# Top-chunk attention and an MLP block on one core: fp16 split selection, constant rows kept in rings, LayerNorm folded into W1, and an order of work written by hand

## The chip, the cores and the metric

The kernel runs on one core of a Trainium2 chip. The metric is the device time of one execution in microseconds (us). TensorE is PE in the profile (its weight loads PEld), VectorE is DVE, ScalarE is ACT, GpSimd is POOL, SyncE is SP. A clock of 1.00 is the full granted clock of TensorE.

## The reference, cut to what matters

There are 4 batches, 8 heads, 768 positions and a head size of 64. Keys are grouped in 24 chunks of 32 positions.

```python
k_min, k_max = min/max of k over each chunk                # per head: 24 x 64
ub = sum_d max(q * k_min, q * k_max)                       # 768 x 24 upper bounds
ub = where(chunk of q >= chunk, ub, -1e9)                  # causal
top = the 6 chunks with the largest ub, for each q
scores = q @ k.T / 8, kept where the key's chunk is in top and key <= query
x = softmax(scores) @ v                                    # heads side by side: 768 x 512
xn = (x - mean(x)) / sqrt(var(x) + 1e-6) * g_ln
out = x + max(xn @ w_ch1, 0) @ w_ch2                       # 512 -> 2048 -> 512
```

Inputs and the output are float32.

## The kernel before

Heads are worked on in pairs; pair g has two heads of one batch, and there are 16 pairs, four to a batch. A pair passes three stages, and then the batch passes a fourth:

- `prep_pair` loads q, k and v, transposes q and k on PE in f32 (L193), and copies q as f32 and as fp16 (L207, L219, L220). It splits q in its positive and its negative part, `Q1` and `Q2` (L223, L224), takes the chunk maxima and minima of k (L213, L214), and puts them in block-diagonal `K1` and `K2`. The fp16 operands `qst` and `kst` of a head have 128 rows: 64 of data, 24 of a chunk mask, and zeros. DVE copies the constant rows anew for each pair (L238 to L245).
- `select_pair` forms the bounds with two f32 matmuls for each of five row tiles (L259, L260; the first 128 rows need no selection). DVE adds the causal bias (L262), finds the largest eight of 24 for each row and head (L269), compares with the seventh (L271), and makes a mask of 0 and -240 (L276). PE transposes the mask (L282, L285) and DVE copies it into the mask rows of `qst` (L288, L289). The score matmul then adds it without another instruction.
- `attend_head` computes the scores transposed, in eight pieces of up to 512 columns (L301), with Exp on ACT (L305). DVE zeroes the upper triangle of the six diagonal blocks (L308), 21 matmuls with v and a column of ones give values and denominators (L313), and DVE normalises (L318, L319).
- `mlp_batch` does LayerNorm row tile by row tile (L331 to L344: statistics, Sqrt on ACT, subtract and scale, transpose), the first product with Relu (L354, L358), the second (L363), the residual add (L368), and the store on POOL's queue (L371).

The weights are loaded and converted by two DMAs on POOL's queue when pair 0 has been prepared, and DVE scales the first by `g_ln` (L153). The outer loop prepares pair g+2, selects pair g+1, attends pair g; when a batch is complete, its MLP follows the attention of the next batch's first pair. Within that, a scheduler orders each engine's instructions. In the shipped order the four scalings of L153 stand in DVE's queue ahead of the rest of the selection of pair 0.

Of the kernel before, what the change touches and what calls it, by code (L numbers as in the profile page):

```python
# [18 lines left out]
def kernel(  # L20
# [9 lines left out]
):  # L30
    nc = tc.nc
# [3 lines left out]
    assert D == 64 and S % P == 0 and H % 2 == 0  # L35
    CH = 32
    NCH = S // CH
    NT = S // P
    HP = H // 2
    SCALE = 1.0 / math.sqrt(D)  # L40
    DM = H * D
    HID = moe_w_ch1.shape[1]
    assert moe_w_ch1.shape[0] == DM and tuple(moe_w_ch2.shape) == (HID, DM)
    KT1 = DM // P
    KT2 = HID // P
    MT1 = HID // P
    LN_EPS = 1e-6
    NEGBIG = -2.0e9
    NEGM = 240.0
    MR = 32  # L50
    assert NCH <= 24 and NT >= 2

    KA = 64 + MR

    const = ctx.enter_context(tc.tile_pool(name="const", bufs=1))
    wpool = ctx.enter_context(tc.tile_pool(name="wpool", bufs=1))
    qkn = ctx.enter_context(tc.tile_pool(name="qkn", bufs=3))
    vp = ctx.enter_context(tc.tile_pool(name="vp", bufs=1))
    pw = ctx.enter_context(tc.tile_pool(name="pw", bufs=3))
    stk = ctx.enter_context(tc.tile_pool(name="stk", bufs=H))  # L60
    vap = ctx.enter_context(tc.tile_pool(name="vap", bufs=3))
    selp = ctx.enter_context(tc.tile_pool(name="selp", bufs=3))
    ptp = ctx.enter_context(tc.tile_pool(name="ptp", bufs=2))
    xp = ctx.enter_context(tc.tile_pool(name="xp", bufs=2))
    lnp = ctx.enter_context(tc.tile_pool(name="lnp", bufs=2))
    xntp = ctx.enter_context(tc.tile_pool(name="xntp", bufs=2))
# [3 lines left out]
    ps_tr = ctx.enter_context(tc.tile_pool(name="ps_tr", bufs=2, space=bass.MemoryType.PSUM))  # L70
    ps_sm = ctx.enter_context(tc.tile_pool(name="ps_sm", bufs=2, space=bass.MemoryType.PSUM))
    ps_sc = ctx.enter_context(tc.tile_pool(name="ps_sc", bufs=3, space=bass.MemoryType.PSUM))
    ps_h = ctx.enter_context(tc.tile_pool(name="ps_h", bufs=1, space=bass.MemoryType.PSUM))

    ident_f = const.tile([P, P], F32, name="ident_f", tag="ident_f")
    make_identity(nc, ident_f)
    ident_h = const.tile([P, P], F16, name="ident_h", tag="ident_h")
    make_identity(nc, ident_h)

    Lmask = const.tile([P, P], F16, name="Lmask", tag="Lmask")  # L80
    nc.gpsimd.memset(Lmask, 1.0)
    nc.gpsimd.affine_select(
        out=Lmask, in_=Lmask, compare_op=ALU.is_ge, fill=0.0,
        base=0, pattern=[[1, P]], channel_multiplier=-1,
    )

    def build_R(tile_rows_base):
        rc = const.tile([tile_rows_base + MR, S], F16, name=f"Rc{tile_rows_base}", tag=f"Rc{tile_rows_base}")
        r = rc[tile_rows_base:tile_rows_base + MR, :]
        nc.gpsimd.memset(r, 0.0)  # L90
        rr = rc[tile_rows_base:tile_rows_base + NCH, :]
        nc.gpsimd.memset(rr, 1.0)
        nc.gpsimd.affine_select(  # L93
            out=rr, in_=rr, compare_op=ALU.is_ge, fill=0.0,
            base=0, pattern=[[1, S]], channel_multiplier=-CH,
        )
        nc.gpsimd.affine_select(
            out=rr, in_=rr, compare_op=ALU.is_ge, fill=0.0,
            base=CH - 1, pattern=[[-1, S]], channel_multiplier=CH,
        )  # L100
        return rc

    Rc64 = build_R(64)
    Rc0 = build_R(0)

    causb = const.tile([P, NT - 1, NCH], F32, name="causb", tag="causb")
    nc.gpsimd.memset(causb, 0.0)
    GPC = P // CH
    for s in range(1, NT):
        for g in range(GPC):  # L110
            nc.gpsimd.affine_select(
                out=causb[g * CH:(g + 1) * CH, s - 1, :],
                in_=causb[g * CH:(g + 1) * CH, s - 1, :],
                compare_op=ALU.is_ge, fill=NEGBIG,
                base=s * GPC + g, pattern=[[-1, NCH]], channel_multiplier=0,
            )

    mneg0 = const.tile([P, MR], F16, name="mneg0", tag="mneg0")
    nc.gpsimd.memset(mneg0, 0.0)
    for g in range(GPC):  # L120
        nc.gpsimd.affine_select(
            out=mneg0[g * CH:(g + 1) * CH, 0:NCH],
            in_=mneg0[g * CH:(g + 1) * CH, 0:NCH],
            compare_op=ALU.is_ge, fill=-NEGM,
            base=g, pattern=[[-1, NCH]], channel_multiplier=0,
        )
    mT0A = const.tile([P, P], F16, name="mT0A", tag="mT0A")
    mT0B = const.tile([P, P], F16, name="mT0B", tag="mT0B")
    ps0 = ps_h.tile([P, 5 * P], F16, name="sel_ps", tag="sel_ps")
    nc.tensor.transpose(ps0[64:64 + MR, 0:P], mneg0, ident_h, tile_position=(0, 64))  # L130
    nc.tensor.transpose(ps0[0:MR, P:2 * P], mneg0, ident_h, tile_position=(0, 0))
    nc.vector.tensor_copy(mT0A[64:64 + MR, :], ps0[64:64 + MR, 0:P])
    nc.vector.tensor_copy(mT0B[0:MR, :], ps0[0:MR, P:2 * P])

    z32 = const.tile([P, S], F16, name="z32", tag="z32")
    nc.gpsimd.memset(z32[0:MR, :], 0.0)

    eps_t = const.tile([P, 1], F32, name="eps_t", tag="eps_t")
    nc.vector.memset(eps_t, LN_EPS)

    wstate = {}

    def load_weights():
        if wstate:
            return
        w1b = wpool.tile([P, KT1, HID], F16, name="w1b", tag="w1b")
        nc.gpsimd.dma_start(w1b, moe_w_ch1.rearrange("(kt p) n -> p kt n", p=P))
        w2b = wpool.tile([P, KT2, DM], F16, name="w2b", tag="w2b")
        nc.gpsimd.dma_start(w2b, moe_w_ch2.rearrange("(kt p) n -> p kt n", p=P))
        gstr = wpool.tile([P, KT1], F32, name="gstr", tag="gstr")  # L150
        nc.sync.dma_start(gstr, moe_g_ln.rearrange("(kt p) -> p kt", p=P))
        for kt in range(KT1):
            nc.vector.tensor_scalar(  # L153
                w1b[:, kt, :], w1b[:, kt, :], gstr[:, kt:kt + 1], None, op0=ALU.mult,
            )
        wstate["w1b"] = w1b
        wstate["w2b"] = w2b
# [6 lines left out]
    def col_chunks(t):  # L164
        res = []
        c0 = P * t
        while c0 < S:
            cw = min(512, S - c0)
            res.append((c0, cw))
            c0 += cw  # L170
        return res

    def prep_pair(b, hp):
        hA = 2 * hp
        qn_t = qkn.tile([P, NT, 2, D], F32, name="qn_t", tag="qn_t")
        kn_t = qkn.tile([P, NT, 2, D], F32, name="kn_t", tag="kn_t")
        for hh in range(2):
            nc.sync.dma_start(qn_t[:, :, hh, :], q_r[b, :, :, hA + hh])
            nc.sync.dma_start(kn_t[:, :, hh, :], k_r[b, :, :, hA + hh])

        qstA = stk.tile([P, S], F16, name="qst", tag="qst")
        qstB = stk.tile([P, S], F16, name="qst", tag="qst")
        kstA = stk.tile([P, S], F16, name="kst", tag="kst")
        kstB = stk.tile([P, S], F16, name="kst", tag="kst")

        def transposes_and_evacs(src_t, stA, stB, fcopy_tile=None, red=None, cast_eng=None):
            cast_eng = cast_eng or nc.vector
            t0 = 0
            while t0 < NT:
                nb = min(4, NT - t0)  # L190
                pst = ps_tr.tile([P, 4 * P], F32, name="tr_ps", tag="tr_ps")
                for tt in range(nb):
                    nc.tensor.transpose(  # L193
                        pst[:, tt * P:(tt + 1) * P], src_t[:, t0 + tt, :, :], ident_f,
                    )
                c0 = t0 * P
                cw = nb * P
                if stA is None:
                    pass
                elif cast_eng is nc.scalar:  # L200
                    nc.scalar.copy(stA[0:64, c0:c0 + cw], pst[0:64, 0:cw])
                    nc.scalar.copy(stB[64:P, c0:c0 + cw], pst[64:P, 0:cw])
                else:
                    cast_eng.tensor_copy(stA[0:64, c0:c0 + cw], pst[0:64, 0:cw])
                    cast_eng.tensor_copy(stB[64:P, c0:c0 + cw], pst[64:P, 0:cw])
                if fcopy_tile is not None:
                    nc.scalar.copy(fcopy_tile[:, c0:c0 + cw], pst[:, 0:cw])  # L207
                if red is not None:
                    kmp, kmn = red
                    cc0 = c0 // CH  # L210
                    ccn = cw // CH
# [36 lines left out]
        for hh in range(2):  # L248
            nc.gpsimd.dma_start(va[:, hh, :, 0:D], v_r[b, :, :, hA + hh])  # L249
# [125 lines left out]
    def get_x_all(bb):  # L375
        if bb not in x_tiles:
            x_tiles[bb] = xp.tile([P, NT, H, D], F16, name="x_all", tag="x_all")
# [76 lines left out]
```

The softmax here doesn't subtract the row's maximum and nothing guards it: scores larger than these inputs give would overflow.

## Time and profile before

| | |
|---|---|
| median of 3 runs | 455.45 us (453.67 to 456.37) |
| profiled execution | the page gives its span, 453.3 us; no other time of it is given |
| mean granted clock of PE | 0.902 |
| busy PE / DVE / ACT / POOL | 368.0 / 261.2 / 208.3 / 69.1 us |
| first score matmul | 45.72 us |
| a pair, without MLP | 13.7 to 13.8 us |
| LayerNorm of batch 0 | 114.5 to 124.3 us |
| MLP products of batch 0 | 124.3 to 144.9 and 144.9 to 166.0 us |

The span runs from the first to the last instruction. Busy times are sums over the span; an engine can be busy for little of the span and still set the pace of one stage, so each stage is read for itself. A line such as `L319 DVE ... x32 | 17.7, 554 | 0.3` says: 32 instructions of source line 319, 17.7 us busy in all, 554 ns for one, and 0.3 us of idle time on that engine just before them.

### The profile page before, as it was taken

Reading aid. Unit: us, or ns where it says so; the run is one execution under the profiler, and the core shown is the slowest. Engines: PE = TensorE matmul, PEld = TensorE weight load, DVE = VectorE, ACT = ScalarE, POOL = GpSimd, SP = SyncE. Lnnn points to the kernel's source line nnn. Section 1 sums busy time; section 2 is a strip of 40 time slices with the busy share of each in tenths; the row PEclk is TensorE's granted clock in tenths of the full one; section 3 lists DMA queues with packets and bytes.
Section 4 is the critical chain, followed back from the end, with each engine's and each line's share of the span. In section 5 each row is a group of like instructions: output and inputs, shape, how many; then the busy total and the mean of one; then the engine's idle time right before and its main releaser. Section 6 shows DMA issues by size and latency. Waiting matters only on the chain.

```text
span 453.3 us, 7365 instructions
## 1 busy us (share of the span) xinstructions
PE 368.0 (81%) x2594; PEld 226.7 (50%) x2594; DVE 261.2 (58%) x967; ACT 208.3 (46%) x512; POOL 69.1 (15%) x167
## 2 busy tenths in 40 slices
PE   2544977888599989888599998877599998759995
PEld 2434645567355446556356445555356445335542
DVE  3568899989840139989850127999850125770011
ACT  3220876654165039854156019865146007816500
POOL 8830102222000111221000111221000110000011
PEclk9999989986599999986579999998579999959999
DMA  9999965345000135554100126220200110000011
GB/s 182 144 207 194 183 91 89 43 62 85 5 0 1 69 98 84 72 82 81 9 0 1 46 74 106 20 18 2 17 0 1 48 69 25 1 1 0 1 69 69
DMA packets 80340, 26.68 MB, mean 59 GB/s; under 512 B 76208, under 2 KB 78256, under 8 KB 80304
## 3 DMA queue, kind: packets, MB, share of 16 engines
q0 software_dynamic: 29600, 13.64, 19.8%
q1 hardware_dynamic: 50704, 12.59, 14.3%
q8 instruction: 20, 0.33, 0.3%
q14 instruction: 16, 0.13, 0.1%
HBM read 27.27 MB, written 6.29 MB: 74 GB/s over the span
## 4 chain that ended last, share of the span: by engine, by line
PE 39%; DVE 25%; issue 22%; POOL 5%; ACT 4%; DMA 3%; POOLq 0%; ACTq 0%
PE sc L354 16%; PE sc L363 10%; ACT pt L305 3%; DMA w1b<-in_moe_w_ch_dram 3%; PE smps L259 3%; PE smps L313 3%; PE smps L260 2%; PE sel_ps L343 2%; DVE m L269 2%; DVE kmp L213 2%; PE sc L301 2%; DVE pt L308 2%; DVE x_all L319 2%; DVE xnT L344 2%; DVE Q L224 1%
## 5 line engine op out<-in xcount | busy, mean ns | idle before, releaser
L305 ACT ACTIVATE pt<-sc 128x512 f16<-128x512 f32 (+3 forms) x256 | 93.5, 478 | 45.1 <-PE sc L301 43.3
L354 PE MATMUL sc<-xnT,w1b 128*128 128x512 f16 (+1 forms) x512 | 94.0, 348 | 2.1 <-DVE xnT L344 2.1
L368 DVE TENSOR_TENSOR ot<-sc,x_all 128x512 f32<-128x512 f32 x24 | 16.6, 692 | 137.1 <-PE sc L363 137.1
L363 PE MATMUL sc<-w2b,hT 128*128 128x512 f16 x384 | 83.5, 379 | 0.0
L301 PE MATMUL sc<-qst,kst 128*128 128x512 f16 (+3 forms) x256 | 67.6, 320 | 14.4 <-ACT pt L305 11.0
L358 ACT ACTIVATE hT<-sc 128x512 f16<-128x512 f32 (+1 forms) x128 | 56.5, 488 | 41.5 <-PE sc L354 41.5
L354 PEld LDWEIGHTS <-w1b 128*128 128x128 f16 x512 | 52.9, 104 | 40.3 <-issue 9.6
L363 PEld LDWEIGHTS <-hT 128*128 128x128 f16 x384 | 37.6, 98 | 44.4
L313 PE MATMUL smps<-va,pt 128*128 128x65 f16 x672 | 45.3, 209 | 10.9 <-DVE pt L308 9.0
L313 PEld LDWEIGHTS <-pt 128*128 128x128 f16 x672 | 33.9, 109 | 36.2 <-DVE pt L308 31.6
L371 POOL DMA_DIRECT2D out_dram<-ot x24 | 13.1, 547 | 223.1 <-DVE ot L368 219.3
L259 PE MATMUL smps<-K,Q 128*128 128x48 f32 x160 | 37.1, 319 | 11.6 <-DVE K L234 10.7
L308 DVE TENSOR_TENSOR pt<-pt,Lmask 128x128 f16<-128x128 f16 x192 | 35.1, 210 | 12.4 <-ACT pt L305 11.4
L301 PEld LDWEIGHTS <-kst 128*128 128x128 f16 x256 | 24.9, 105 | 27.9 <-issue 22.5
L260 PE MATMUL smps<-K,Q 128*128 128x48 f32 x160 | 37.0, 318 | 0.0
L259 PEld LDWEIGHTS smps<-K,Q 128*128 128x128 f32 x160 | 30.1, 234 | 12.9 <-issue 12.9
L249 POOL DMA_DIRECT2D va<-in_v_dram x32 | 28.2, 886 | 46.1 <-PE smps L313 32.4
L305 ACT ACT_TABLE_LOAD x3 | 3.8, 1283 | 63.1 <-PE sc L301 63.1
L343 PE MATMUL sel_ps<-ident_h,xn 128*128 128x128 f16 x96 | 14.7, 308 | 19.5 <-DVE xn L338 16.7
L260 PEld LDWEIGHTS smps<-K,Q 128*128 128x128 f32 x160 | 30.3, 236 | 0.0
L193 PE MATMUL tr_ps<-ident_f,qn_t 128*128 128x128 f32 x96 | 20.4, 326 | 10.5 <-POOL Rc L93 5.6
L207 ACT COPY qTf<-tr_ps 128x512 f32<-128x512 f32 (+1 forms) x32 | 15.4, 542 | 22.6 <-PE tr_ps L193 22.6
(77 smaller groups left out, 405.6 us busy)
## 6 DMA issues: line engine op xcount, KB each, us to landing
qn_t<-in_q_dram SPq DMA_DIRECT2D x32, 192.0 KB, 3.6
kn_t<-in_k_dram SPq DMA_DIRECT2D x32, 192.0 KB, 3.6
out_dram<-ot POOLq DMA_DIRECT2D x24, 256.0 KB, 2.3
va<-in_v_dram POOLq DMA_DIRECT2D x32, 96.0 KB, 3.2
w1b<-in_moe_w_ch_dram POOLq DMA_DIRECT2D x1, 2048.0 KB, 14.4
w2b<-in_moe_w_ch_dram POOLq DMA_DIRECT2D x1, 2048.0 KB, 27.0
gstr<-in_moe_g_ln_dram SPq DMA_DIRECT2D x1, 2.0 KB, 3.7
```

Source lines behind the costliest of these rows:

```text
L193: nc.tensor.transpose(pst[:, tt * P:(tt + 1) * P], src_t[:, t0 + tt, :, :], ident_f,)
L249: nc.gpsimd.dma_start(va[:, hh, :, 0:D], v_r[b, :, :, hA + hh])
L259: nc.tensor.matmul(ub_ps[:, s - 1, :], Q1[:, s * P:(s + 1) * P], K1, start=True, stop=False)
L260: nc.tensor.matmul(ub_ps[:, s - 1, :], Q2[:, s * P:(s + 1) * P], K2, start=False, stop=True)
L301: nc.tensor.matmul(sc[:, 0:cw], kst[0:rows, t * P:(t + 1) * P], qst[0:rows, c0:c0 + cw], start=True, stop=True,)
L305: nc.scalar.activation(ptt[:, c0 - P * t:c0 - P * t + cw], sc[:, 0:cw], ACTF.Exp, scale=SCALE,)
L308: nc.vector.tensor_tensor(ptt[:, 0:P], ptt[:, 0:P], Lmask, ALU.mult)
L313: nc.tensor.matmul(pv_ps[:, s, 0:D + 1], PT[t][:, (s - t) * P:(s - t + 1) * P], va[:, hh, t, 0:D + 1], start=(t == 0), stop=(t == s),)
L343: nc.tensor.transpose(pxn[:, kt * P:(kt + 1) * P], xn[:, kt * P:(kt + 1) * P], ident_h)
L354: nc.tensor.matmul(hp[:, 0:cw], w1b[:, kt, m * P:(m + 1) * P], xnT[:, kt, c0:c0 + cw], start=(kt == 0), stop=(kt == KT1 - 1),)
L358: nc.scalar.activation(ht[:, c0:c0 + cw], hp[:, 0:cw], ACTF.Relu)
L363: nc.tensor.matmul(yp[:, 0:DM], hT[kt][:, s * P:(s + 1) * P], w2b[:, kt, :], start=(kt == 0), stop=(kt == KT2 - 1),)
```

## The change

The kernel is written anew around the same mathematics.

- **Order.** Each step is a function, put in a list with a time counted in pairs, and all are issued in the order of these times; each engine runs its instructions in that order. Score pieces of pair g start at g, its first preparation is at g - 1.98, its selection at g - 0.97. The MLP of batch b takes four pairs of the next batch: 32 pieces of the first product in two pairs, 24 of the second in the next two.
- **Selection in fp16.** q times 128 is split in a high part `qh` (ACT) and a rest `ql` (DVE); `rh` and `rl` are their positive parts. Chunk minima and max minus min are split the same way. Four fp16 matmuls of 96 columns replace two f32 ones of 48, and DVE adds the two halves in two steps.
- **Rings.** Three sets of fp16 operands stand fixed. The mask matrix sits once in the constant rows of `KA` and `KB`; mask rows that are not needed stay zero.
- **Packed bins.** The score columns of a head go in six bins of up to 512 columns, so ACT has six Exp instructions for eight. One DVE instruction masks the six diagonal blocks.
- **LayerNorm.** W1 is scaled by `g_ln`, and the mean of its rows is taken off it once, so x itself is transposed and multiplied. The factor 1/std, from POOL's pow, is applied in the last add. The statistics stay on DVE.
- **Queues.** Weights are loaded in eight DMAs on POOL's queue; outputs leave on SP's queue, which also loads q and k.
- **PSUM.** Transposes have one f32 tile of two banks, fp16 transposes one bank, bounds and values two, and scores, both MLP products and the W1 mean share three.

```diff
+    def prep_q(g):
...
+        for t in range(NT):
+            nc.tensor.transpose(pst[:, t * P:(t + 1) * P], qn[:, t, :, :], ident_f)
...
+        nc.scalar.activation(qh, pst, ACTF.Copy, scale=QS)
+        nc.vector.scalar_tensor_tensor(
+            ql, pst[:, P:S], QS, qh[:, P:S], op0=ALU.mult, op1=ALU.subtract,
+        )
+        nc.vector.tensor_scalar_max(rh, qh[:, P:S], 0.0)
+        nc.vector.scalar_tensor_tensor(
+            rl, qh[:, P:S], 0.0, ql, op0=ALU.is_gt, op1=ALU.mult,
+        )
+        nc.vector.tensor_copy(QA[g % NR][0:64, :], qh[0:64, :])
+        nc.vector.tensor_copy(QB[g % NR][64:P, :], qh[64:P, :])
...
+    def prep_k(g):
...
+        nc.vector.tensor_reduce(kc[:, 0, :], view, axis=AX.X, op=ALU.min)
+        nc.vector.tensor_reduce(kx, view, axis=AX.X, op=ALU.max)
+        nc.scalar.copy(KA[g % NR][0:64, :], pst[0:64, :])
+        nc.scalar.copy(KB[g % NR][64:P, :], pst[64:P, :])
...
+    def bounds(g):
...
+        for s in range(NT - 1):
+            o = ub[:, s].rearrange("p l h c -> p (l h c)")
+            stats = [(p["qh"], P, 0), (p["ql"], 0, 0), (p["rh"], 0, 1), (p["rl"], 0, 1)]
+            for i, (a, off, arr) in enumerate(stats):
+                c0 = off + s * P
+                nc.tensor.matmul(
+                    o, a[:, c0:c0 + P], bd[:, arr].rearrange("p l h c -> p (l h c)"),
+                    start=(i == 0), stop=(i == 3),
+                )
...
+    def select(g):
...
+        nc.vector.tensor_tensor(
+            ubt, ub[:, :, 1], causb.unsqueeze(2).to_broadcast([P, NT - 1, 2, NCH]), ALU.add,
+        )
+        nc.vector.tensor_tensor(ubm, ub[:, :, 0], ubt, ALU.add)
...
+    def mask_t(g):
...
+            nc.tensor.transpose(pm[:, s * P:(s + 1) * P], mn[:, s, :], ident_h)
+        nc.vector.tensor_copy(QA[g % NR][64:P, P:S], pm[64:P, 0:SB0])
+        nc.vector.tensor_copy(QB[g % NR][0:64, P:S], pm[0:64, 0:SB0])
+
+    BINS = [
+        [(0, 0, 512)], [(1, 128, 640)], [(0, 512, 768), (4, 512, 768)],
+        [(2, 256, 768)], [(3, 384, 768)], [(1, 640, 768), (5, 640, 768)],
+    ]
...
+    def x_t(g):
...
+            nc.tensor.transpose(
+                px[:, s * P:(s + 1) * P],
+                x_all[:, s, 2 * hp:2 * hp + 2, :].rearrange("p h d -> p (h d)"), ident_h,
+            )
+        nc.vector.tensor_copy(xT[:, hp, :], px)
...
+        if j == 3:
...
+            nc.vector.scalar_tensor_tensor(
+                ot, yp, rs[b][1][:, s:s + 1], x_all[:, s].rearrange("p h d -> p (h d)"),
+                op0=ALU.mult, op1=ALU.add,
+            )
+            nc.sync.dma_start(out_r[b, s], ot)
...
+    for g in range(NG):
+        at(max(g - 3.0, -8.0 + 0.1 * g) if g > 2 else -8.0 + 0.1 * g, lambda g=g: load_qk(g))
+        at(g - 2.8, lambda g=g: load_v(g))
+        at(g - 1.98, lambda g=g: prep_q(g))
+        at(g - 1.60, lambda g=g: prep_k(g))
+        at(g - 0.98, lambda g=g: bounds(g))
+        at(g - 0.97, lambda g=g: select(g))
+        at(g - 0.45, lambda g=g: mask_t(g))
+        for i in range(6):
+            at(g + 0.065 * i, lambda g=g, i=i: score_bin(g, 0, i))
+            at(g + 0.42 + 0.065 * i, lambda g=g, i=i: score_bin(g, 1, i))
+        for hh in range(2):
+            t0 = g + 0.42 * hh
+            at(t0 + 0.36, lambda g=g, hh=hh: diag(g, hh))
+            for j in range(3):
+                at(t0 + 0.50 + 0.06 * j, lambda g=g, hh=hh, j=j: values(g, hh, 2 * j, 2 * j + 2))
+            at(t0 + 0.66, lambda g=g, hh=hh: normalise(g, hh))
+        at(g + 1.17, lambda g=g: x_t(g))
+    for i in range(NR):
+        at(-2.5 + 0.01 * i, lambda i=i: consts_ring(i))
+    for kt in range(KT1):
+        at(-0.6 + 0.25 * kt, lambda kt=kt: w1_load(kt))
+        at(1.55 + 0.3 * kt, lambda kt=kt: w1_scale(kt))
+        at(2.75 + 0.2 * kt, lambda kt=kt: w1_mean(kt))
+        at(3.50 + 0.2 * kt, lambda kt=kt: w1_center(kt))
+        at(0.6 + 0.4 * kt, lambda kt=kt: w2_load(kt))
+    for b in range(B):
+        e = 4.0 * (b + 1) + 0.2
...
+            at(e + 0.25 + 0.1 * s, lambda b=b, s=s: stats(b, s))
...
+                at(e + 0.05 + 2.0 * n / 32, lambda b=b, m=m, half=half: mlp1(b, m, half))
...
+                at(e + 2.06 + 2.0 * n / 24, lambda b=b, s=s, j=j: mlp2(b, s, j))
...
+    with tc.manual_schedule():
+        for _, _, fn in sorted(pieces, key=lambda x: x[:2]):
+            fn()
```

`consts_ring` copies the mask matrix `RT`, built once on POOL, into the constant rows of the rings. `diag` is the one masking multiplication of a head, `values` the 21 value matmuls, `normalise` the division by the denominators, `w1_center` the subtraction of the mean from one of W1's four parts.

## The prediction

> **What bounds the kernel now.** I read the page, then a table of stretches, the chain of waits for the start, the groups by shape, and the timeline. On the page, PE has no stage of its own below half load except the start, and DVE alternates between 9 and 0.
>
> ```profile
> span 453.3 us, 7365 instructions
> ...
> PE 368.0 (81%) x2594; PEld 226.7 (50%) x2594; DVE 261.2 (58%) x967; ACT 208.3 (46%) x512; POOL 69.1 (15%) x167
> ...
> PE   2544977888599989888599998877599998759995
> ...
> DVE  3568899989840139989850127999850125770011
> ...
> PEclk9999989986599999986579999998579999959999
> ```
>
> The shares are averages over stages, so the stages come next (columns: window, length, busy us of PE, PEld, DVE, ACT, POOL, granted clock, DMA share, GB/s): a pair of heads, the LayerNorm, the first and the second MLP product.
>
> ```profile
> 73.20:87.00 13.80, 10.89 (x101) 7.59 (x100) 12.49 (x52) 8.52 (x24) 2.73 (x6) 0.88 0.49 73
> ...
> 114.50:124.30 9.80, 5.86 (x30) 3.45 (x31) 8.58 (x27) 1.79 (x6) 0.00 (x0) 0.50 0.00 0
> 124.30:144.90 20.60, 20.60 (x125) 12.35 (x124) 5.91 (x29) 13.61 (x31) 0.00 (x0) 0.97 0.00 1
> 144.90:166.00 21.10, 21.10 (x107) 9.61 (x106) 3.85 (x6) 0.42 (x2) 2.75 (x5) 1.00 0.16 63
> ```
>
> A pair lasts 13.8 us and DVE fills 12.5 of it; LayerNorm is DVE too; the MLP is PE alone at full clock with DVE idle. Two engines take turns. Before the first score (45.7 us) the chain holds a DMA that DVE waits for:
>
> ```profile
> 20.21 14.45 DMA w1b<-in_moe_w_ch_dram
> 34.68 2.74 DVE w1b L153 x4
> ```
>
> **The change, part by part.** Durations come from these groups (last figures: busy, mean ns of one, idle before) and, for runs of matmuls, from the timeline (start, length).
>
> ```profile
> L319 DVE TENSOR_TENSOR x_all<-smps,rden 128x384 f16<-128x384 f32 x32 | 17.7, 554 | 0.3
> L207 ACT COPY qTf<-tr_ps 128x512 f32<-128x512 f32 x16 | 10.2, 639 | 22.6 <-PE tr_ps L193 22.6
> L269 DVE MAX8 m<-ubm 128x8 f32<-128x24 f32 x160 | 14.9, 160 | 0.1
> L262 DVE TENSOR_TENSOR ubm<-smps,causb 128x240 f32<-128x240 f32 x16 | 6.2, 390 | 0.3 <-PE smps L260 0.3
> ```
> ```profile
> 75.31 0.88 PE L193 MATMUL tr_ps<-ident_f,kn_t 128*128 128x128 f32 x6 [0.76 <-ACT qTf L207]
> 381.17 0.38 PE L313 MATMUL smps<-va,pt 128*128 128x65 f16 x7
> ```
>
> PE work of a pair at full clock: 42 value matmuls at 0.03 (seven in 0.38, 0.2 of it drain) 1.3; score columns 5,376 at the MLP's rate (20.72 us for 96 of 512) 2.3; 12 f32 transposes at 0.11, 1.3; 20 f16 bounds matmuls of 96 columns, which the trace does not show: between the f16 value row's 0.03 and 0.22 of the f32 row they replace (the ten take 2.2), taken at 0.045, near the row of their own type: 0.9, at the most 4.4; 5 mask and 6 x transposes 0.6. Sum 6.4. The MLP adds (20.6 + 20.7)/4 = 10.35 per pair: 16.75.
>
> DVE work of a pair falls from 12.5 to about 11.4. Out: six constant-row copies (L238 to L243, 0.36 each), two of 0.2, Q1 and Q2 (0.59 + 0.73), four K copies (0.17 each). In: ql, rh, rl, a second add, five small bound operations (0.17 each). Twelve Lmask products of 128 (six in 0.88) become two of 768, 0.6 each. Of LayerNorm the statistics stay (6 x 0.84 a batch, in the slack of pair 4); its normalising pass, copies and 24 Sqrt with their table loads (four of 1.28, and three back to Exp) go, and one rstd factor enters the last add. ACT gets 12 exps a pair for 16, some 0.12 of fixed time saved on each (the eight of a head now take 2.85), beside PE. Folding the mean costs 16 matmuls of 512 on PE (16 x 0.216 = 3.5), in batch 0 where PE waits anyway, and four centers on DVE.
>
> If engines only had to be fed, PE would set 16.75. But the order is written out, and I followed one pair through it. On PE: bounds(g+1), prep_q(g+2), the last values of g-1, a few bins and MLP tiles, then x_t(g-1). On DVE: ql, rh, rl and two copies of g+2, then select(g+1), then normalise(g-1). So x_t waits for all of them. With time 0 at bounds: 0.9 bounds, 0.88 transposes, qh on ACT 0.83 (0.639 + 0.193 for 256 more columns, from the two L207 shapes) = 2.65. DVE: ql 0.83 (384 in 0.554 and 512 in 0.692 give 1.08 ns per element), rh 0.33 (between L276's 0.21 for 240 and L153's 0.75 for 2,048), rl 0.33 to 0.67 (that rate, or five of L308's 0.134), taken at 0.5 in the middle, copies 0.70, two adds 0.78, ten MAX8 0.93, compare 0.40, reciprocal and multiply 0.76: 5.2. x_t can start at 7.85. PE has until then 0.9 + 0.65 + 0.35 + 0.42 and one or two MLP tiles, 3.2 to 3.6. It stalls 4.2 to 4.6 us in every pair. Queued behind x_t on PE are bins 3 to 5 of this head, so its exps, diag, prep_k and the whole next head. The later waits have cover in MLP pairs: diag(g,0) ends near 11.6 and its values come at 12.7; diag(g,1) near 18.4, values at 19. Period 16.75 + 4.4 = 21.15.
>
> Sums:
> - Start. DVE ring copies wait for POOL's RT (two masked strips of 0.73 + 0.82 + 0.99 after 3 us) to about 8.6, then 2.5; prep_q 2.4, prep_k's reduces and bins to 16.4; bounds, prep_q(1), select(0), prep_k(1), mask in that order to 29.5, PE at half rate. The w1 scale moves behind the start of pair 1, about 50 us in, so its DMA is hidden (both weights landed within 27 us of issue). Gain 16.
> - Batch 0 has no MLP to fill in, so the chain itself is the period, part of it at half clock: 8.3 to x_t, its transposes, three bins and their exps to 10.4, diag 0.6, two reduces 1.8 (0.67 and 0.41 for 512 and 256), bound operations 0.95, mask copies 0.95 (L288, L289), normalise 0.76, diag 0.6 to 16.1, values and the next bin to 16.9. Pair 0 has no x_t: 13.5. 13.5 + 3 x 16.9 + four scales 3.0 + three centers at 1.3 (between L153's 0.75 and sixteen of L308's 0.134) = 71. Here the new order is slower than the old (13.8 a pair).
> - Pairs 4 to 15: 12 x 21.15 = 254, less 10 since the last two have no prep or bounds: 244.
> - End: 3.5 for the last x_t, 41.3 MLP, 4.3 from last matmul to the end as now: 49.
>
> Total 393.5, before the clock. Costed at nothing: stores on SP ahead of q/k loads, which run one to two pairs (over 20 us) ahead against 3.6 to land, and POOL's pow, which no row shows (0 to 3 us) and which has a pair of slack; without that cover each would cost its landing once a batch.
>
> **The clock.** These 1 us windows show PE going idle at 395.2 after the last values:
>
> ```profile
> 397.00:398.00 1.00, 0.00 (x0) 0.00 (x0) 1.00 (x4) 0.48 (x2) 0.00 (x0) 1.00 0.00 0
> 398.00:399.00 1.00, 0.00 (x0) 0.00 (x0) 0.96 (x4) 0.00 (x0) 0.00 (x0) 0.77 0.00 0
> ...
> 408.00:409.00 1.00, 1.00 (x4) 0.36 (x3) 0.00 (x0) 0.38 (x1) 0.00 (x0) 0.61 0.00 0
> ```
>
> The clock halves 3.0 us after PE stopped, and returns 3.6 us after dense work began at 405 (4.2 at 226.9). A stall of 4.4 is longer than that, so I expect each to be followed by 3.5 to 4 us at half clock, a loss of 1.8: 11 x 1.8 = 20. Total 413.5; the median lies 2.15 above the profiled span now, so 415.7.
>
> The Trainium skill ("TensorE: Matmul & The Clock Gate", section "HAM oscillation — how this bites in real kernels") asks for no PE gap over about 3.4 us and speaks against this order. Its window would give 1.7 per stall, 19 in all; the rows give 20.
>
> **The rivals.**
> Feeding nearly suffices (0.17): DVE's operations overlap more than I allow (MAX8 says 160 ns of one, but ten take 0.93), the stall falls to 2 and the clock holds: 393.5 - 11 x 2.4 = 367 for the span; with the stall but no clock loss 393.5. For it: in 168 to 193 the clock never fell under gaps of 0.7 us. Against: the order is strict.
> More hand-overs wait (0.09): 2 us more on each of 16 pairs, 448.
> Slower than before (0.08): after the stall the clock does not recover within the pair. For it: in 225.3 to 231 and 105 to 113 it stayed at half for 6 to 8 us though PE was busy. Against: whole MLP stages ran at 1.00, and MLP tiles fill these pairs. A pair at half clock costs 0.5 us per us spent there; above (453.3 - 393.5)/12 = 5.0 per pair, so 10 us of half clock in each, it decides; 6 per pair give 467.
> That the change doesn't spread the load (DVE still the bound beside the MLP) is priced by DVE's 11.4 + 2.3 for statistics and stores against 16.75 of PE: no time of its own.
>
> **How the numbers follow.** Forecast case (0.66): 416, own range 395 to 437. The range 380 to 447 takes the unknown rl, centers, bounds, half of the better case and most of the third. A measurement can tell 0.5% (2.3 us). Faster 0.90 (all but the slow case and a sliver), same 0.02, slower 0.08.
>
> **What would show it.** PE waiting for DVE at x_t, 4 us in each of pairs 4 to 13, the clock at 0.5 after it; first score at 29; batch 0 pairs near 17; pairs with MLP near 23; one table load on ACT. Wrong if PE has no such gap (then 370 to 393), or if the longest wait is another one.

## The result, and the profile after

The changed kernel takes 466.47 us (median of 4 runs, 465.05 to 467.48) where the kernel before, in the runs beside it, takes 455.87 (453.67 to 456.37). The ratio is 1.0251, 95% interval 1.0215 to 1.0288: 2.5% slower. The forecast was 416, range 380 to 447, with 0.90 on faster.

The page of after, same rows as shown of before:

```profile
span 464.1 us, 6459 instructions
...
PE 329.0 (71%) x2528; PEld 203.1 (44%) x2528; DVE 231.7 (50%) x645; ACT 192.3 (41%) x373; POOL 46.9 (10%) x79
...
PE   1544565645686777869676796858579679999996
...
DVE  3667557566665435464566325456555533435011
...
PEclk9996667877797898989789797989879889999999
```

PE does 39 us less busy work (329.0 for 368.0) and DVE 30 less, yet the span is 10.8 longer. No engine alternates between 9 and 0 any more: PE stands mostly at 5 to 8 and DVE at 4 to 6, and the clock row, mostly 9 outside LayerNorm before, is at 6 and 7 in batch 0 and dips to 7 and 8 all the way to the last MLP. Two half-loaded engines with a sagging clock suggest hand-overs, not a full engine. The stages (columns as before: window, length, busy us of PE, PEld, DVE, ACT, POOL, granted clock, DMA share, GB/s) are batch 0, four pairs from one selection to the next (two beside the first MLP product, two beside the second), and the end:

```profile
29.80:109.60 79.80, 44.17 (x407) 32.20 (x405) 50.23 (x140) 34.16 (x64) 6.79 (x11) 0.73 0.58 88
116.90:144.20 27.30, 19.53 (x161) 12.44 (x161) 17.10 (x49) 14.98 (x30) 3.42 (x4) 0.87 0.18 22
144.20:173.50 29.30, 21.61 (x165) 14.00 (x165) 11.38 (x35) 15.47 (x31) 1.80 (x3) 0.83 0.11 8
173.50:197.80 24.30, 18.20 (x149) 10.83 (x149) 12.82 (x36) 8.76 (x16) 1.79 (x3) 0.93 0.34 63
197.80:222.80 25.00, 18.57 (x149) 10.65 (x149) 13.60 (x38) 8.38 (x15) 1.79 (x3) 0.93 0.37 73
417.00:464.00 47.00, 42.87 (x234) 22.54 (x234) 10.56 (x21) 13.95 (x32) 1.32 (x1) 0.98 0.11 40
```

PE is idle 6 to 8 us in each of the pairs, at a clock of 0.83 to 0.93; in the end, where the MLP is alone, it is busy for 42.9 of 47. What PE and ACT wait for (us in total, times, longest):

```profile
PE trh L346 <- DVE x_all L337: 62.8, 14, 5.8
...
ACT KA L232 <- DVE kx L231: 52.1, 16, 9.0
...
PE mm L383 <- ACT pt L306: 19.6, 6, 3.3
```

The first row is the wait that the prediction named. The other two belong together in the six pairs beside a first product, and it named neither. The timeline of such a pair shows both waits of PE (start, length; in brackets the idle time before and its releaser). Its bounds begin at 138.26:

```profile
138.26 0.21 PE L251 MATMUL sm<-BD,qh 128*128 128x96 f16 x1
...
140.83 0.82 DVE L211 SCALAR_TENSOR_TENSOR ql<-tr,qh 128x640 f16<-128x640 f32 x1 [3.29 <-ACT qh L210]
...
144.15 0.95 DVE L268 MAX8 m<-ubm 128x8 f32<-128x24 f32 x10
...
145.69 0.56 DVE L337 TENSOR_TENSOR x_all<-sm,rden 128x384 f16<-128x384 f32 x1
146.30 0.82 PE L346 MATMUL trh<-ident_h,x_all 128*128 128x128 f16 x6 [4.28 <-DVE x_all L337]
...
152.01 0.56 DVE L313 TENSOR_TENSOR pt<-pt,Lmask 128x768 f16<-128x768 f16 x1 [4.29 <-ACT pt L306]
...
154.04 0.95 DVE L231 TENSOR_REDUCE kx<-tr 128x24 f32<-128x768 f32 x1
...
155.08 0.79 ACT L232 CAST KA<-tr 64x768 f16<-64x768 f32 x1 [1.97 <-DVE kx L231]
...
155.88 0.79 ACT L233 CAST KB<-tr 64x768 f16<-64x768 f32 x1
...
156.70 0.60 ACT L306 ACTIVATE pt<-mm 128x512 f16<-128x512 f32 x1
...
157.35 1.02 PE L383 MATMUL mm<-xT,w1b 128*128 128x512 f16 x4 [3.26 <-ACT pt L306]
...
184.71 0.38 PE L297 MATMUL mm<-QB,KB 128*128 128x256 f16 x2 [1.43 <-DVE ot L403]
```

Follow it downwards. `x_t` starts 8.04 us after the bounds (forecast 7.85) and PE has stood 4.28 (forecast 4.2 to 4.6). That part is as written. Then the late scores make the exps late, DVE's triangle mask (L313) waits 4.29 for them, and DVE's two chunk reductions of the next k stand behind it and end at 154.99. ACT's copies of the same PSUM tile into `KA` and `KB` stand behind those reductions: ACT, with an Exp and a Relu queued behind it and 1.97 us idle, copies only from 155.08 to 156.67. Meanwhile the three PSUM buffers that scores and MLP share fill up, and PE stands a second time, 3.26 us. (The last row is of a pair beside the second product. There the second wait is 1.43 us; the profile puts its end down to DVE's last add, `ot`, which stands behind the same reductions.) The clock falls twice:

```profile
144.00:145.00 1.00, 0.00 (x0) 0.00 (x0) 0.97 (x11) 0.00 (x0) 0.00 (x0) 0.88 0.81 51
145.00:146.00 1.00, 0.00 (x0) 0.00 (x0) 0.93 (x5) 0.00 (x0) 0.00 (x0) 0.50 0.00 0
151.00:152.00 1.00, 1.00 (x7) 0.57 (x6) 0.00 (x0) 0.78 (x3) 0.00 (x0) 0.70 0.00 0
...
157.00:158.00 1.00, 0.65 (x4) 0.29 (x4) 0.00 (x0) 1.00 (x3) 0.00 (x0) 1.00 0.00 0
158.00:159.00 1.00, 1.00 (x10) 0.86 (x9) 0.00 (x0) 0.65 (x3) 0.00 (x0) 0.71 0.00 0
161.00:162.00 1.00, 1.00 (x11) 0.56 (x9) 0.50 (x2) 0.46 (x1) 0.00 (x0) 0.58 0.00 0
```

A mean of 0.88 in a window that starts at 1.00 puts the fall at 144.76, 2.7 us after PE stopped at 142.02; 0.70 puts the return at 151.6. So PE runs at half speed for 5.3 us from its restart at 146.30. The second wait ends at 157.35 and the clock falls after it, at 158.4, and is back at 161.8: 3.4 us at half, 1.7 lost where PE is busy throughout.

Set side by side by the starts of the selections (the first MAX8 of a pair), the two kernels differ thus: up to the first selection -12.9 us (37.3 to 24.4), the next five selections, without MLP, +25.9 (66.6 to 92.5), the next four, which hold one MLP, +3.3 (102.6 to 105.9), the rest -5.6. Over a batch in the middle the gains of the new order and its waits nearly cancel.

### The profile page after: what moved, and what is told of

Read it like the earlier page. It is cut to its first block, busy times and chain, and to the rows that moved or that the text cites. A ratio compares the mean times of both kernels' runs of the same rounds, so it can differ in the third digit from the quotient of the medians.

```text
span 464.1 us, 6459 instructions
## 1 busy us (share of the span) xinstructions
PE 329.0 (71%) x2528; PEld 203.1 (44%) x2528; DVE 231.7 (50%) x645; ACT 192.3 (41%) x373; POOL 46.9 (10%) x79
## 4 chain that ended last, share of the span: by engine, by line
PE 57%; DVE 29%; ACT 10%; issue 2%; POOL 1%; ACTq 0%; POOLq 0%
PE mm L383 18%; PE mm L396 17%; PE mm L297 6%; PE sm L251 4%; PE sm L326 4%; DVE m L268 3%; DVE kc L230 3%; DVE kx L231 3%; ACT pt L306 3%; DVE ql L211 3%; PE tr L205 3%; ACT qh L210 3%; PE trh L346 3%; DVE rl L215 3%; DVE x_all L337 2%
## 5 line engine op out<-in xcount | busy, mean ns | idle before, releaser
L306 ACT ACTIVATE pt<-mm 128x512 f16<-128x512 f32 (+1 forms) x192 | 98.8, 544 | 91.8 <-PE mm L297 90.5
L383 PE MATMUL mm<-xT,w1b 128*128 128x512 f16 (+1 forms) x512 | 110.2, 358 | 20.4 <-ACT pt L306 19.6
L396 PE MATMUL mm<-w2b,hT 128*128 128x512 f16 x384 | 98.9, 396 | 1.0 <-ACT pt L306 0.5
L387 ACT ACTIVATE hT<-mm 128x512 f16<-128x512 f32 (+1 forms) x128 | 60.0, 490 | 71.8 <-PE mm L383 71.6
L346 PE MATMUL trh<-ident_h,x_all 128*128 128x128 f16 x96 | 11.9, 287 | 62.8 <-DVE x_all L337 62.8
L297 PE MATMUL mm<-QB,KB 128*128 128x512 f16 (+3 forms) x128 | 35.0, 336 | 17.4 <-ACT pt L306 11.0
L326 PE MATMUL sm<-va,pt 128*128 128x65 f16 x672 | 39.4, 203 | 7.3 <-DVE pt L313 7.3
L313 DVE TENSOR_TENSOR pt<-pt,Lmask 128x768 f16<-128x768 f16 x32 | 17.8, 557 | 52.9 <-ACT pt L306 52.9
L297 PE MATMUL mm<-QA,KA 128*128 128x512 f16 (+3 forms) x128 | 38.5, 371 | 3.7 <-DVE QA L279 2.6
L403 DVE SCALAR_TENSOR_TENSOR ot<-mm,rstd,x_all 128x512 f32<-128x512 f32 x24 | 18.0, 749 | 44.5 <-PE mm L396 44.5
L297 PEld LDWEIGHTS <-KB 128*128 128x128 f16 x128 | 12.9, 106 | 16.9 <-issue 10.4
L205 PE MATMUL tr<-ident_f,qn 128*128 128x128 f32 x96 | 16.8, 323 | 4.7 <-DMA qn<-in_q_dram 4.7
```

The lines of the kernel that those rows point to most:

```text
L205: nc.tensor.transpose(pst[:, t * P:(t + 1) * P], qn[:, t, :, :], ident_f)
L297: nc.tensor.matmul(sc[:, o:o + c1 - c0], ks[:, t * P:(t + 1) * P], qs[:, c0:c1], start=True, stop=True,)
L306: nc.scalar.activation(dst, sc[:, 0:o].rearrange("p (a c) -> p a c", a=len(segs)), ACTF.Exp, scale=SCALE / QS,)
L326: nc.tensor.matmul(pv[:, s, 0:D + 1], flat[:, c0:c0 + P], va[:, hh, t, 0:D + 1], start=(t == 0), stop=(t == s),)
L346: nc.tensor.transpose(px[:, s * P:(s + 1) * P], x_all[:, s, 2 * hp:2 * hp + 2, :].rearrange("p h d -> p (h d)"), ident_h,)
L383: nc.tensor.matmul(hp_[:, 0:cw], w1b[:, kt, m * P:(m + 1) * P], xT[:, kt, c0:c0 + cw], start=(kt == 0), stop=(kt == KT1 - 1),)
```

## The experiments

Theory: PE stands twice in a pair, each time because an instruction that is wanted now was issued behind one that is not: `x_t` behind `prep_q` and `select` on DVE, and Exp behind the K copies, which wait for DVE's reductions of the same tile. Rivals: one of the waits hides the other; the clock, not the waits, is the loss; PE or DVE is full whatever the order.

**The K copies ahead of the reductions**, and nothing else:

```diff
+        nc.scalar.copy(KA[g % NR][0:64, :], pst[0:64, :])
+        nc.scalar.copy(KB[g % NR][64:P, :], pst[64:P, :])
         nc.vector.tensor_reduce(kc[:, 0, :], view, axis=AX.X, op=ALU.min)
         nc.vector.tensor_reduce(kx, view, axis=AX.X, op=ALU.max)
-        nc.scalar.copy(KA[g % NR][0:64, :], pst[0:64, :])
-        nc.scalar.copy(KB[g % NR][64:P, :], pst[64:P, :])
```

> Against the changed kernel (464.1 us span): in prep_k the two ACT copies of the transposed k stand ahead of the two DVE reductions that read the same PSUM tile; nothing else changes. Theory A (ACT's copies wait for DVE's reductions, and Exp and Relu queue behind them, so the score buffers run out and PE stops): the wait of L383 and L297 for ACT and the second clock dip go, 3.3 + 1.7 in each of six pairs with the first MLP product, 1.4 in six with the second, 4 in each of three pairs of batch 0: 464 falls to about 415 to 428. DVE's reductions wait 1.6 longer instead. Theory B (the excess over the forecast is the clock alone, and the ACT wait only shows where PE would have been slow anyway): 455 or more.

Measured 445.9 us, ratio to before 0.9806 (0.9771 to 0.9841); 20.6 below after. The gain is there, but half of what was expected. PE's waits in this run:

```profile
PE trh L346 <- DVE x_all L337: 62.3, 14, 5.8
...
PE mm L383 <- ACT pt L306: 8.1, 6, 1.3
```

The second wait falls from 19.6 to 8.1 us in six pairs, not to nothing: ACT still spends 1.6 us on the copies with Exp behind them. And the first wait is untouched. The order now holds the other way: DVE's reductions wait for ACT's copies (timeline of this run).

```profile
153.85 0.96 DVE L232 TENSOR_REDUCE kc<-tr 128x24 f32<-128x768 f32 x1 [2.25 <-ACT KB L231]
```

**`x_t` freed of `prep_q` and `select`**: DVE's part of `prep_q` is issued a quarter of a pair later and `select` 0.12 later, so that both stand behind `normalise` and `x_t`.

```diff
         at(g - 1.98, lambda g=g: prep_q(g))
+        at(g - 1.98 + 0.25, lambda g=g: prep_q2(g))
...
-        at(g - 0.97, lambda g=g: select(g))
+        at(g - 0.97 + 0.12, lambda g=g: select(g))
```

`prep_q2` holds the five DVE instructions of `prep_q`.

> Against the changed kernel: DVE's part of prep_q (ql, rh, rl, two copies) and select come after normalise of the pair before, so x_t waits for normalise alone. Same instructions. Theory A (each of the two waits costs by itself): the 4.3 to 4.7 us stall before x_t and the half clock after it go, about 6 in each of ten pairs and 3 in batch 0: 390 to 405. Theory B (the stall only moves, since DVE is behind by the same work and the score bins of the next head wait for mask and reductions): 440 to 464.

Measured 397.82 us, ratio 0.8736 (0.8703 to 0.8769), 68.7 below after. This is the larger of the two losses. In the two traces, whose spans differ by 65.3, the first selection comes 4.6 earlier, 9.6 lie in batch 0 (from the first to the sixth selection 82.9 us for 92.5) and 51 behind it, in the pairs beside MLP pieces, for which the forecast charged (4.4 + 1.8) x 11 = 68.

**Both:**

> Both reorderings. If the two waits are separate causes, the gains add: about 365 to 385, PE near 17 us per pair with MLP and the clock near 1.00 from pair 5 on. If they share the same time, no better than the better one of the two alone.

Measured 372.51 us, ratio 0.8184 (0.816 to 0.8208), 94 below after, where the two edits alone give 20.6 and 68.7. They add, with 5 more, so neither wait hid the other. The page of this kernel, and two of its pairs:

```profile
PE   1156556586558989999979899999898999999995
...
PEclk9999887769699999999999999999999999999999
```
```profile
124.30:143.80 19.50, 17.76 (x169) 11.95 (x167) 11.20 (x35) 15.12 (x32) 2.02 (x4) 1.00 0.16 11
161.20:179.00 17.80, 17.19 (x150) 10.06 (x149) 13.10 (x38) 8.44 (x16) 1.77 (x4) 1.00 0.52 101
```

From the first MLP on PE is at 8 or 9 in the row and the clock never dips. A pair beside the second product is now 17.8 us with 17.19 of PE, which is the bound there; beside the first product 1.7 us of 19.5 are still idle.

**The clock by itself.** 64 transposes of a constant, whose result is overwritten, stand on PE ahead of the `x_t` of pairs 4 to 13, which runs one pair later; the order on DVE and ACT stays, and `x_t` starts 8.0 us after the bounds as before.

```diff
+        if 4 <= g <= 13:
+            for i in range(64):
+                nc.tensor.transpose(px[:, (i % NT) * P:(i % NT + 1) * P], Lmask, ident_h)
```

> The changed kernel with 64 more fp16 transposes of a constant (3.5 us at full clock) on PE just ahead of x_t's own in the ten pairs 5 to 14; they fill the time in which PE waits for normalise, and their output is overwritten. If the half clock after the stall costs what the trace suggests (1.7 in pairs with the second product, 3.0 with the first): 440 to 450. If the clock costs nothing: 464, or a little more where the extra transposes outlast the wait.

Measured 455.61 us, ratio 1.0007 (0.9983 to 1.0031): 10.9 below after, for work that computes nothing. The same stretch after `x_t` in a pair beside the second product, after (two lines) and with the added transposes:

```profile
200.00:201.00 1.00, 1.00 (x7) 0.75 (x8) 0.15 (x1) 0.00 (x0) 0.00 (x0) 0.50 0.08 16
201.00:202.00 1.00, 1.00 (x4) 0.42 (x3) 0.40 (x1) 0.00 (x0) 0.00 (x0) 0.50 0.00 0
```
```profile
198.00:199.00 1.00, 1.00 (x11) 0.53 (x8) 0.56 (x1) 0.00 (x0) 0.00 (x0) 1.00 0.00 0
...
200.00:201.00 1.00, 0.95 (x6) 0.47 (x6) 0.00 (x0) 0.38 (x1) 0.00 (x0) 1.00 0.18 68
```

Keeping the clock up after `x_t` gained 1.1 us per pair net of the added work (10.9 over ten pairs); the forecast charged 1.8. The second wait and its dip remain in this run.

**Which of the two moved parts held `x_t`?** First only `prep_q`'s DVE part late, then only `select` late:

```diff
 first
+        at(g - 1.98 + 0.25, lambda g=g: prep_q2(g))
 second
-        at(g - 0.97, lambda g=g: select(g))
+        at(g - 0.97 + 0.12, lambda g=g: select(g))
```

> The changed kernel with only the five DVE instructions of prep_q (ql, rh, rl, two copies) issued a quarter of a pair later, behind x_t; select stays ahead of normalise. Theory (x_t waits because DVE works off, in its order, prep_q's part, which itself waits for qh): what is left ahead of x_t is bounds 0.9, select 2.1 and normalise 0.76, 3.8 us against 3.6 of PE's own work, so the stall before x_t falls from 4.3 to under 0.7 and the time to 395 to 410 us, as with both moved (397.8). Rival (select is what x_t waits for): little moves, 450 to 466. If the two weigh alike: 425 to 440.

> The changed kernel with only select moved behind normalise and x_t; prep_q's DVE part stays. Theory (a sum along DVE's queue): x_t starts at 2.65 (qh) + 2.8 + 0.76 = 6.2 after bounds instead of 8.0, PE has 3.6, the stall is 2.6 in place of 4.3. That is 1.7 by 14 pairs = 24 us, and if a wait under 3 us leaves the clock alone, up to 1.8 by 11 more: 423 to 443 us. Rival (select alone is what x_t waits for): 395 to 410. Rival (prep_q alone, select without weight): 460 to 466.

Measured 392.93 us (ratio 0.8641, 0.8616 to 0.8665) and 431.21 (0.9468, 0.9445 to 0.949). PE's wait before `x_t` in each:

```profile
PE trh L349 <- DVE x_all L340: 10.2, 14, 1.3
```
```profile
PE trh L349 <- DVE x_all L340: 33.6, 13, 3.6
```

62.8 us became 10.2 and 33.6. The first is a little better than both moved together (397.82): with `select` early, batch 0 takes 76.9 us for 82.9, from the first to the sixth selection. The sum along DVE's queue comes out in the second run, 2.6 us a pair (33.6 over 13) where 2.6 was worked out, and is half a microsecond short in the first, 0.7 (10.2 over 14) where 0.2 was. The larger part is `prep_q`: its first DVE instruction waits for `qh` from ACT (3.29 us of DVE idle in the timeline above), which waits for PE's transposes, and all that is ready stands behind it.

The second of these runs also tells something of the clock. Its expectation allowed that a wait under 3 us might leave the clock alone. Here PE stood 2.11 us before its `x_t` at 138.18:

```profile
137.00:138.00 1.00, 0.00 (x0) 0.00 (x0) 0.93 (x3) 0.00 (x0) 0.01 (x1) 1.00 1.49 102
138.00:139.00 1.00, 0.82 (x11) 0.78 (x12) 0.93 (x4) 0.00 (x0) 0.00 (x0) 1.00 0.74 47
139.00:140.00 1.00, 1.00 (x5) 0.35 (x3) 0.97 (x11) 0.84 (x2) 0.00 (x0) 0.55 0.00 0
...
142.00:143.00 1.00, 1.00 (x7) 0.61 (x6) 0.00 (x0) 0.81 (x3) 0.00 (x0) 0.74 0.00 0
```

The clock falls at 139.1, with PE busy again for almost 1 us, and returns at 142.5. But in the same trace a wait of the same length, up to 164.46, left no dip, nor did two of its three waits of 2.55 us. The length of a wait alone does not decide; the last section comes back to this.

**The MLP not spread**, on the kernel with both repairs:

```diff
-            at(e + 0.25 + 0.1 * s, lambda b=b, s=s: stats(b, s))
+            at(e + 0.001 * s, lambda b=b, s=s: stats(b, s))
...
-                at(e + 0.05 + 2.0 * n / 32, lambda b=b, m=m, half=half: mlp1(b, m, half))
+                at(e + 0.05 + 0.0001 * n, lambda b=b, m=m, half=half: mlp1(b, m, half))
...
-                at(e + 2.06 + 2.0 * n / 24, lambda b=b, s=s, j=j: mlp2(b, s, j))
+                at(e + 0.06 + 0.0001 * n, lambda b=b, s=s, j=j: mlp2(b, s, j))
```

The statistics of LayerNorm move ahead with the MLP pieces.

> The kernel with both repairs (372.5 us), but the 56 MLP pieces of a batch issued in one go after the first pieces of the next batch's first pair, not spread over four pairs. Theory (spreading fills PE while DVE and ACT work on a pair): a pair without MLP then lasts about 16.5 as in batch 0, and each MLP 41: 29.8 + 12 + 13 x 16.5 + 2 x 12 + 4 x 41 + 8 = 452, less some overlap of the clusters with the next preparation: 430 to 455 us. Rival (any order will do that keeps x_t and the K copies free): under 385.

Measured 458.25 us, ratio 1.0064 (1.0042 to 1.0086), 3 above the expected range. A pair without MLP and one with a whole MLP:

```profile
163.00:179.10 16.10, 10.03 (x104) 7.42 (x103) 11.08 (x36) 7.95 (x15) 2.00 (x4) 0.79 0.40 60
104.00:163.00 59.00, 51.11 (x322) 29.13 (x322) 20.41 (x54) 21.50 (x46) 2.30 (x3) 0.94 0.27 60
```

16.1 us with PE at 10.0 and a clock of 0.79, then 59 of which PE works 51. Spreading is worth 86 us, once the waits are gone.

**The start.** The kernel before, with the scaling of W1 called behind pair 2:

```diff
         do_attend(g)
+        if g == 2:
+            scale_weights()
```

> The kernel before, with the four scalings of W1 called behind pair 2 and nothing else moved; the scheduler then places them after the third selection. Theory (the start of the old kernel waits for the load of W1): the first score comes near 30 us for 45.7, and the four scalings add up to 3.0 us in a stretch where DVE is nearly full: 439 to 443 us. Rival (the start is bound by the chain of pairs 0 and 1 in any case): 452 to 456.

Measured 449.69 us, ratio 0.9897 (0.9856 to 0.9939). The expectation missed: the first score comes at 40.4 us, not near 30, for 45.5 (the first score matmul in the trace of before starts at 45.51; the table of before has 45.72). The load of W1 held the old start by 5 us, not by 16. The other 11 us by which the new kernel starts earlier must come from the rest of the change, order, constants and selection together; they were not taken apart.

**Towards a better version.** `KB`'s copy on DVE behind the reductions; `prep_q` late with the copies first; the same with the copies first only from pair 5 on; and both repairs with `select` early in pairs 0 to 4 alone. In that order, each as an edit of the kernel with both repairs, except the third, which is shown against the changed kernel, where the copies come last (its `prep_q` is late and its `select` early as in the second):

```diff
-        nc.scalar.copy(KB[g % NR][64:P, :], pst[64:P, :])
...
+        nc.vector.tensor_copy(KB[g % NR][64:P, :], pst[64:P, :])
```
```diff
-        at(g - 0.97 + 0.12, lambda g=g: select(g))
+        at(g - 0.97, lambda g=g: select(g))
```
```diff
+        if g >= 5:
+            nc.scalar.copy(KA[g % NR][0:64, :], pst[0:64, :])
+            nc.scalar.copy(KB[g % NR][64:P, :], pst[64:P, :])
...
+        if g < 5:
+            nc.scalar.copy(KA[g % NR][0:64, :], pst[0:64, :])
+            nc.scalar.copy(KB[g % NR][64:P, :], pst[64:P, :])
```
```diff
-        at(g - 0.97 + 0.12, lambda g=g: select(g))
+        at(g - (0.97 if g < 5 else 0.85), lambda g=g: select(g))
```

> The kernel with both repairs (372.5 us), with the copy into KB moved from ACT to DVE, behind the two reductions. Theory (the 1.34 us that PE still waits for ACT in pairs with the first MLP product comes from 1.6 us of K copies with Exp and Relu queued behind them): the burst is 0.8, the wait falls to about 0.5, in six pairs about 5 us, and the other pairs stand: 363 to 370 us. Rival (DVE's longer work of 0.8 per pair is what counts): 372 to 385.

> The changed kernel with prep_q's DVE part late (392.9 us by itself) and the K copies ahead of the reductions; select stays at its place. Theory (the two waits are separate and add): the copies gave 25 us on top of the version with both parts late (397.8 to 372.5), so 392.9 - 25 = 368; batch 0 keeps the shorter pairs that an earlier select gave it (59.3 for 63.6 us): 365 to 371 us. Rival (an early select takes the place of a K reduction that the copies now have to precede): 372 to 380.

> As the run beside it, but the K copies stand ahead of the reductions only from pair 5 on, whose preparation lies beside MLP pieces; in pairs 0 to 4 the reductions stay first. Theory (in batch 0 DVE's chain sets the period, and reductions that wait 1.6 us for two copies lengthen it, while nothing urgent queues on ACT): some 1 us less in each of pairs 0 to 2, 362 to 369 us. Rival (in batch 0 as well Exp waits behind the copies): no less than the run beside it.

> The version with both repairs (372.5 us), with select of pairs 0 to 4 back at its first place ahead of normalise and select of the other pairs left behind x_t. Theory (in the last four versions two small effects cancel: an early select shortens the pairs of batch 0, where the sixth selection came at 96.9 for 103.8 us in the runs before, and lengthens the pairs beside MLP pieces by 0.4 to 1.4, where x_t waits 0.6 us for it): with each taken where it helps, 372.5 less up to 6.9: 364 to 369 us. Rival (the pairs that follow give back what batch 0 gains, since the MLP waits for all of batch 0's x and PE is behind by then): 371 to 374.

Measured 371.37 (ratio 0.8159, 0.8134 to 0.8183), 373.44 (0.8201, 0.8162 to 0.824), 373.3 (0.8202, 0.8158 to 0.8246) and 369.03 us (0.8117, 0.8082 to 0.8153). The first three missed the gains expected of them, against 372.51. With `KB` on DVE, PE's wait for ACT shrinks as expected, but another grows:

```profile
PE sm L329 <- DVE pt L316: 18.6, 11, 5.5
PE tr L229 <- DVE ql L215: 8.3, 4, 3.4
PE mm L386 <- ACT pt L309: 8.1, 6, 1.3
```
```profile
PE sm L329 <- DVE pt L316: 25.2, 15, 6.5
PE tr L229 <- DVE ql L215: 14.3, 5, 6.0
...
PE mm L386 <- ACT pt L309: 2.5, 6, 0.4
```

8.1 became 2.5, but 18.6 + 8.3 became 25.2 + 14.3. By pair, from bounds to bounds: of those beside a first product, one in two is 0.9 us shorter (18.49 for 19.42) and the other 0.2 longer, those beside a second product are 0.3 to 0.4 longer, and batch 0 (first to sixth selection) is 0.6 longer; DVE now spends 0.96 us on the copy in every pair. In the next two, `select` ahead of `x_t` lets batch 0 end sooner (the sixth selection at 96.9 and 97.8 for 103.8 us) and makes `x_t` wait 0.6 us a pair in the first of them (8.9 us in 14 places), and gain and loss cancel; where the copies stand in batch 0 made no difference (373.44 and 373.3). Taking each where it helps gives the last, 369.03, the fastest, at the upper edge of its expectation; its interval lies just below that of the kernel with both repairs (0.816 to 0.8208) and overlaps that with `KB` on DVE.

## Why the prediction was wrong

Where the forecast's terms went (its sum was 413.5 with the clock; the profiled span is 464.1, so 50.6 are missing):

| stage | forecast | measured |
|---|---|---|
| to the first score | 29.5 | 29.2 to 29.8 (first matmul, first exp) |
| batch 0 | 71 | 79.8 |
| pairs 4 to 15, clock included | 264 | 307.4 |
| end | 49 | 47.1 |

- **Right: the wait at `x_t`.** 7.85 worked out from rows of before, 8.04 found; stall 4.2 to 4.6 against 4.27 to 4.72 in eight of the ten pairs with MLP pieces and 5.1 in two. That each such stall is followed by the half clock was right too; the fall came 2.6 to 5.1 us after PE stopped, not always at 3.
- **The step that failed: "The later waits have cover in MLP pairs".** It compared DVE's triangle masks with PE's values and looked no further (and even those came later: `diag(g,0)` ended 14.3 us after the bounds, where 11.6 was worked out). It left out that ACT's copies into `KA` and `KB` read the tile that DVE reduces, stand behind those reductions, and have Exp and Relu queued behind them on ACT. It is a hand-over of the kind of the rival "more hand-overs wait", priced there at 2 us a pair and given 0.09. The edit that takes only this away gave 20.6 us on its own and 25.3 on top of the other repair. It is not the whole miss: that run, at 445.9, is still 30 above the forecast. Over pairs 4 to 13 (22.95 x 10 = 229.5 forecast) the changed kernel takes 274.7 us and that run 252.8, so the edit removes about half of what these pairs are over.
- **By pair.** Forecast 21.15 + 1.8 = 22.95. Beside the second product the pairs take 24.3 to 25.4: PE's own work is 17.2 for 16.75 (as the run with both repairs shows it at full clock), and a second wait of 1.43 is added, which that run no longer has; the two come to 1.9 of the 1.4 to 2.4 us that these pairs are over. The pair that begins at 138.26 takes 29.34, 6.4 over: PE's work 17.8, 1.0 over; the second wait 3.26; its dip 1.7; and the first dip 2.65 (5.3 at half) for 1.8, 0.85 over. The terms come to 6.8. Six pairs at about 6 and four at about 2 make the 43 that pairs 4 to 15 are over.
- **A rule that bore on the failed step.** In none of these runs do DVE's reduction and ACT's copy of one PSUM tile overlap, whichever stands first (1.97 us of ACT idle in one order, 2.25 of DVE in the other). The Trainium skill ("PSUM — Partial Sum Buffer", section "PSUM bank collisions raise a hardware error") says that two engines may not read the same bank and quadrant at once; the prediction did not draw on it.
- **The clock term** was 20 us, 1.8 after each stall. The added transposes took back 10.9 at the first wait; the second dip was not taken away by itself. After the ten stalls the clock stayed at half for 3.41 us in four and for 6.83 in six. Two readings behind the term are off: the windows shown put the fall at 398.54, 3.4 us after PE's last work ended at 395.15, not 3.0, and the return at 408.78, 3.8 us after 405, not 3.6.
- **Batch 0** was 8.8 short. Copies first do not shorten it (from the first to the sixth selection 92.0 us for 92.5), `prep_q` late does (76.9). That points to the same queue on DVE: the wait at `x_t` is 5.76 us in pair 1, where no MLP piece fills it. How much of the 8.8 is the clock (0.73 over the batch) was not separated.
- **Sizes and sums.** `rl` took 0.82 where 0.5 was taken, 0.3 of the 8.04; the bounds matmuls (0.042 for 0.045) and the W1 centers (1.21 for 1.3) were close. DVE's work of a pair does not add up: the listed terms take 12.5 to 10.3, not 11.4 (a pair without MLP pieces had 11.1 in the run with the MLP not spread). POOL's two strips end at 8.1 by the sum, not 8.6, and the three terms up to `qh` make 2.61, not 2.65. None of these decides.
- **The start** was right as a number, 16 us, by luck: the run with W1's scaling late gave 5 of them.
- **The rivals.** "Feeding nearly suffices" (367 to 393): the repaired orders reach its number, 369 to 373, but by moving instructions, not because DVE's operations overlap more. That "the clock does not recover within the pair" is not what made it slower, though its price, 467, is the time measured: beside MLP pieces the clock recovered each time, after at most 6.83 us. DVE beside MLP pieces is busy 11.4 to 17.1 us in pairs of 24 to 30, so it is not the bound there.

The verdict's sign hung on little: 0.90 on faster rested on a period of 23 us against a break-even near 26 (22.95 plus 39.8, the distance from 413.5 to 453.3, over 12 pairs), and one unseen wait with its dip lifted six pairs past it.

## What to carry to other kernels

In an order written by hand, list for every step all of its instructions on every engine, and ask of the first one on each queue what it waits for: an instruction that waits for another engine must not stand ahead of one that is ready and that the bounding engine wants. Follow a stall past its first victim, round the loop through each engine, until something with slack takes it up; here the second turn, DVE to ACT to PE, decided the sign. In these runs two engines that read one PSUM tile ran one behind the other, in the order of the program; count it as a dependence.

## What the runs showed of the hardware and was not expected

- Useless work can pay: 64 transposes (20.6 us more of busy PE) made the kernel 10.9 us faster, with the clock at 1.00 and not 0.50 after the wait.
- The clock moves in steps. In every trace here a stretch at half clock that ends within it lasts a whole multiple of 3.41 us (144.76 to 151.6, 158.4 to 161.8 and 139.1 to 142.5 above are two steps, one and one), and all of a trace begin on one grid of that step. So the time from a stop of PE to the fall, and from its restart to the return, depends on where in a step they lie.
- A wait of 2.11 us can be enough for a dip, and the fall then comes after PE is at work again; the length of the wait does not decide. The Trainium skill ("TensorE: Matmul & The Clock Gate", section "HAM oscillation — how this bites in real kernels") gives as a rule no gap over about 3.4 us. In the run with `select` late, three of five waits of 2.11 to 2.13 us were followed by a dip; in the changed kernel, four of six of 3.26. What goes with the dips is how long PE was busy within a step: the 2.11 us up to 138.18 lie in one step (135.69 to 139.11, PE busy 1.31 of 3.42), those up to 164.46 in two (2.76 and 1.86 busy, no dip). Beside MLP pieces, in these two traces, the clock fell after steps with PE busy up to 0.38 of the time and held after those with 0.40 or more.
- `scalar_tensor_tensor` on 640 elements a partition took the same 0.82 us whether its input is f32 in PSUM (`ql`) or all fp16 in SBUF (`rl`); the `tensor_scalar` between them takes 0.32 for as many:

```profile
141.57 0.32 DVE L214 TENSOR_SCALAR rh<-qh 128x640 f16<-128x640 f16 x1
...
141.81 0.82 DVE L215 SCALAR_TENSOR_TENSOR rl<-qh,ql 128x640 f16<-128x640 f16 x1
```
